# Loading a weight matrix by three transfers over 128 partitions instead of four over 32

## The chip, the cores and the metric

The kernel runs on one core of a Trainium2 chip. A core has five engines that run side by side: TensorE (PE) multiplies matrices, VectorE (DVE), ScalarE (ACT) and GpSimd (POOL) work on elements, and SyncE (SP) issues transfers. Each has its own list of instructions, worked off in order; semaphores hold one until another's result is there. Data lie in a memory of 128 partitions (SBUF). Transfers between it and the main memory (DRAM) are carried out by 16 DMA engines, which all issuing engines share. The metric is the device time of one execution in microseconds (us).

## What is computed

A gated linear attention runs over 4 x 8 sequences of 768 steps with heads of 48; its output, as 3072 tokens of 384, goes through a feed-forward block with two weights, 384 x 2048 and 2048 x 384:

```python
for t in range(S):
    state = alpha[:, :, t, :, None] * state + np.einsum('bhd,bhe->bhde', k[:, :, t], v[:, :, t])
    y[:, :, t] = np.einsum('bhd,bhde->bhe', q[:, :, t], state)
x = y.transpose(0, 2, 1, 3).reshape(B * S, H * D)
h = x @ w_in
g = h * np.clip(h + 3.0, 0.0, 6.0) / 6.0
out = g @ w_out
```

q, k, v and alpha are float32. Both weights are float64, so each of their numbers is moved as two 32-bit words, and the kernel makes float32 of them on the chip.

## The kernel before

The 3072 tokens are 24 chunks of 128 (six per batch), and two chunks are a group. For a chunk the kernel loads alpha, k, q and v (lines 263 to 297), makes running products of alpha (lines 335 and 346), scores, the part within the chunk and the part from the state (lines 395 to 544), and puts the result, transposed, into xT (line 546). For a group the feed-forward block follows: from group 2 on by the products of a fast matrix scheme (line 685 for the first weight, line 785 for the second), in the first two groups in the plain way, because the weights are still coming in: ff1 (line 559, matmuls in line 564) and ff1_half (line 568, line 575) for the first weight, ff2 (line 597, line 602) for the second.

The order of all steps is written out by hand as one long string of words (from line 831 on); a word is a step's short name with its arguments, and each engine gets its instructions in that order. `w.i` is load_weight(i), `d1.i`, `d2.i`, `dx.i`, `d3.i` and `d4.i` decode a slice (round_low on ACT, line 207; magnitude on ACT, line 217; sign on ACT, line 212; high_bits on DVE, lines 224 to 231; add_low on POOL, line 238), `f.g.i.m` is ff1 of group g on the first weight's slice i, and `fa`, `fb` are its two halves. `la`, `lk`, `lq` and `lv` load alpha, k, q and v of a chunk.

Each weight comes in eight slices (NSL = 768 numbers for each of 128 partitions). Slices 0 to 7 are the first weight: slice i is its columns 256 i to 256 i + 255, all 384 rows. The row 96 p + 32 t + r (p under 4, t under 3, r under 32) belongs in partition 32 p + r, place t; a piece of a row is 256 numbers of 8 bytes, 2 KB in one run. A slice lands in a raw buffer (five for these slices, used in turn, HOMES in line 162), is decoded into w1, and the buffer is loaded again. Slices 8 to 15 are the second weight, with 128 partitions in one transfer of 3 KB runs (line 187).

All these loads are issued by SP, in the written order. From the first slice to the last of the first weight it is: w.1, the loads lq.2, lk.2 and lk.3, w.0, lq.3 and lv.2 (two transfers), w.3, w.4, w.5, w.2, la.5, lq.5, la.4 and lv.4 (two transfers), w.6, w.7; then lq.4 and the second weight from w.8 on. Some wait: w.5 until POOL has used the buffer of slice 0, w.7 until it has used that of slice 2, lk.3, lv.2, lq.5 and lv.4 until PE is done with the old contents. Each transfer also counts on one of eight semaphores in turn, and waits for the transfer eight before it, which used the same one. On PE the first uses of the slices come in the order 1, 0, 3, 4, 2, 5, 6, 7; after `f.1.5.0` and a transpose the order is

```
f.1.0.3 f.1.6.2 f.1.7.0 f.0.7.3 f.0.6.2
```

and after these the second weight is used, from `b.1.0` on.

Of the kernel before, what the change touches and what calls it, by code (L numbers as in the profile page):

```python
# [17 lines left out]
def kernel(  # L18
# [32 lines left out]
    nc = tc.nc  # L51
# [5 lines left out]
    NP = H // 2  # L57
    DF = moe_w_out.shape[0]
    KT = DM // C
# [38 lines left out]
    for r in range(max(NR, NV)):  # L98
        for name, pad, n in (("a", 1.0, NR), ("k", 0.0, NR), ("q", 0.0, NR), ("v", 0.0, NV)):
            if r >= n:  # L100
                continue
            if name == "v":
                t = consts.tile([C, H, 64], FP, tag=f"v{r}")
            else:
                t = rings[:, 3 * r + "akq".index(name)]
# [12 lines left out]
    for r in range(2):  # L118
        t = consts.tile([C, NP * W + 1], FP, tag=f"ax{r}")
        nc.vector.memset(t, 0.0)  # L120
        aX.append(t)
        t = consts.tile([C, NP * W], FP, tag=f"ini{r}")
# [8 lines left out]
    for r in range(2):  # L131
        t = consts.tile([C, NP, 2 * D], FP, tag=f"st{r}")
        nc.gpsimd.memset(t, 0.0)
        st.append(t)
    for r in range(2):
        t = consts.tile([C, NP, 2 * D], FP, tag=f"sm{r}")
# [27 lines left out]
    def raw_of(i):  # L164
        return raws[HOMES[i]]

    def weight_dst(i):
        if i < NW1:
            n = NSL // KT
            return w1[:, :, i * n : (i + 1) * n]  # L170
        m = NSL // DM
        return w2[:, (i - NW1) * m : (i - NW1 + 1) * m, :]

    def load_weight(i):
        u = 2 if wide else 1
        dst = weight_dst(i)
        m = dst.shape[1]
        to = raw_of(i).rearrange("p (m n) w -> p m (n w)", m=m) if wide else dst
        if i < NW1:
            n = NSL // KT  # L180
            src = moe_w_in[:, u * i * n : u * (i + 1) * n].rearrange(
                "(p t r) f -> p r t f", p=NP, t=KT)
            for p in range(NP):
                nc.sync.dma_start(out=to[32 * p : 32 * p + 32], in_=src[p])
        else:
            o = (i - NW1) * m * C
            nc.sync.dma_start(
                out=to, in_=moe_w_out[o : o + m * C, :].rearrange("(f p) n -> p f n", p=C))
# [468 lines left out]
    for i in range(8):  # L657
        r, o = divmod(i, 3)
# [70 lines left out]
    t = {1: b[0, 1], 2: spare[:, 0], 3: spare[:, 1], 4: spare[:, 2]}  # L729
# [73 lines left out]
    def store2(g, i):  # L803
# [6 lines left out]
    steps = {  # L810
        "la": lambda j: load_akq("a", j), "lk": lambda j: load_akq("k", j),
        "lq": lambda j: load_akq("q", j), "lv": load_v, "w": load_weight,
        "d1": round_low, "d2": magnitude, "dx": sign, "d3": high_bits, "d4": add_low,
        "ta": lambda j: transposed("a", j), "tk": lambda j: transposed("k", j),
# [182 lines left out]
```

## Time and profile before

| | |
|---|---|
| median of 3 runs | 563.11 us (562.15 to 563.6) |
| the profiled execution, its own time | 562.15 us |
| its span, first to last instruction | 560.4 us |
| PE busy in 0 to 10, 10 to 20, 20 to 30 us | 8.54, 9.36, 9.20 us |
| PE busy in each 10 us from 30 to 110 us | 10.00 us |
| first weight: transfers in the trace | 24 to raw buffers, 8 to a buffer that lies in g_sb, 192 KB each |
| one issue of them on SP, median | 428 ns (311 to 1811) |
| from issue to landing, median | 4.6 us (3.3 to 6.5) |
| all transfers from 10 to 56 us | 9.11 MB, 198 GB/s, 92% of 16 engines |

The page gives each engine's busy time, then the span in 40 slices of 14 us, in which a digit is the busy share in tenths. A row of a timeline is start, duration, engine, line and operation, and in brackets how long the engine stood before it and what ended that. A row of windows is a stretch, its length, the busy time (and count) of PE, of PE's weight loads, DVE, ACT and POOL, then the granted clock of TensorE (1.00 is full), the mean busy share of the DMA engines and GB/s. A row of DMA packets is their count and bytes; behind the queue's name stand packets, MB and the time that the packets took as a share of 16 engines over the stretch. Packets of one engine can overlap, so that share can pass 100%. "SPq" is SP's queue of transfers.

### The profile page before, as it was taken

To read this page: it belongs to the slowest core of one execution; us is meant where nothing else is said; L and a number is where in the kernel's file an instruction comes from. 1 tells how busy PE (TensorE), PEld (TensorE's weight loads), DVE (VectorE), ACT (ScalarE), POOL (GpSimd) and SP (SyncE) were. 2 spreads that over 40 slices of the span, in tenths; PEclk is the share of its full clock that TensorE was granted. 3 is DMA by queue.
4 is the path that set the end of the run, shared out by engine and by line. 5 is a ranking of instruction groups with operands and counts; after the bars stand their busy time and mean duration, and the time that the engine had idled before them with its cause. 6 is when DMAs were issued, how large, how long until landed. Compare 5 with 4: busy or idle time off the path is not lost.

```text
span 560.4 us, 14913 instructions
## 1 busy us (share of the span) xinstructions
PE 548.9 (98%) x6222; PEld 511.3 (91%) x6222; DVE 470.3 (84%) x822; ACT 210.3 (38%) x382; POOL 55.1 (10%) x76
## 2 busy tenths in 40 slices
PE   8999999999999999999999899999999999999997
PEld 8789876799899899999999799999999999999997
DVE  6979897999999899999998589999789777484570
ACT  2676671104523424322333242442333422542420
POOL 3343346000000000000000000000100100000000
PEclk9999999999999999999999999999999999999999
DMA  8997679311305344445424544253125040000000
GB/s 175 211 205 177 187 225 209 87 36 30 90 8 138 89 96 96 111 117 113 133 59 107 122 109 103 70 137 80 48 65 114 4 126 1 9 15 15 9 15 29
DMA packets 98516, 52.83 MB, mean 94 GB/s; under 512 B 51472, under 2 KB 91664, under 8 KB 98448
## 3 DMA queue, kind: packets, MB, share of 16 engines
q1 hardware_dynamic: 91824, 47.15, 35.9%
q10 hardware_dynamic: 6624, 4.72, 2.6%
q8 instruction: 49, 0.80, 0.6%
q14 instruction: 19, 0.16, 0.1%
HBM read 43.71 MB, written 8.13 MB: 93 GB/s over the span
## 4 chain that ended last, share of the span: by engine, by line
PE 80%; DVE 8%; SPq 5%; DMA 4%; issue 2%; ACT 0%; POOL 0%; DVEq 0%; ACTq 0%; POOLq 0%
PE m_ps L785 30%; PE m_ps L685 26%; PE m_ps L564 6%; PE m_ps L602 4%; SPq L292 2%; PE m_ps L575 2%; PE y_ps L543 2%; SPq L277 2%; PE sc_ps L377 1%; DMA kq<-in_k_dram 1%; PE y_ps L523 1%; PE sc_ps L402 1%; PE m_ps L617 1%; SPq L460 1%; PE y_ps L527 1%
## 5 line engine op out<-in xcount | busy, mean ns | idle before, releaser
L785 PE MATMUL m_ps<-w,g_sb 128*128 128x192 f32 x704 | 121.8, 327 | 1.2 <-DVE g_sb L626 0.8
L785 PEld LDWEIGHTS m_ps<-w,g_sb 128*128 128x128 f32 x704 | 113.8, 190 | 2.7 <-DVE g_sb L626 1.0
L691 ACT COPY g_sb<-m_ps 128x512 f32<-128x512 f32 x110 | 64.2, 584 | 127.7 <-PE m_ps L685 121.3
L785 PE MATMUL m_ps<-rings,g_sb 128*128 128x192 f32 x528 | 92.6, 329 | 0.0
L685 PE MATMUL m_ps<-xc,w 128*128 128x128 f32 x640 | 84.2, 279 | 2.9 <-DVE oh L801 2.5
L785 PEld LDWEIGHTS m_ps<-rings,g_sb 128*128 128x128 f32 x528 | 86.6, 193 | 0.2 <-DVE g_sb L626 0.2
L580 ACT ACTIVATE r<-g_sb,half 128x512 f32<-128x512 f32 x80 | 57.2, 722 | 69.0 <-DVE g_sb L626 29.1
L685 PEld LDWEIGHTS m_ps<-xc,w 128*128 128x128 f32 x640 | 78.1, 192 | 5.3 <-DVE oh L801 2.7
L584 DVE SCALAR_TENSOR_TENSOR g_sb<-r,g_sb 128x512 f32<-128x512 f32 x80 | 55.4, 697 | 12.1 <-ACT r L580 8.4
L465 POOL TENSOR_TENSOR t<-t,R 128x384 f32<-128x384 f32 x20 | 19.9, 994 | 368.9 <-DVE t L503 137.5
L685 PE MATMUL m_ps<-xT,raw 128*128 128x128 f32 x400 | 52.9, 277 | 0.0
L685 PEld LDWEIGHTS m_ps<-xT,raw 128*128 128x128 f32 x400 | 49.2, 192 | 0.5
L685 PE MATMUL m_ps<-xT,w 128*128 128x128 f32 x320 | 43.5, 281 | 0.0
L732 DVE TENSOR_TENSOR g_sb<-g_sb 128x512 f32<-128x512 f32 (+1 forms) x55 | 41.7, 789 | 0.2
L685 PEld LDWEIGHTS m_ps<-xT,w 128*128 128x128 f32 x320 | 38.9, 191 | 1.8 <-ACT g_sb L691 0.2
L622 DVE TENSOR_TENSOR g_sb<-g_sb 128x512 f32<-128x512 f32 x40 | 26.9, 680 | 12.3 <-ACT g_sb L691 12.1
L564 PE MATMUL m_ps<-xT,w 128*128 128x256 f32 x144 | 32.3, 381 | 0.0
L685 PE MATMUL m_ps<-xc,raw 128*128 128x128 f32 x240 | 32.1, 278 | 0.0
L335 DVE TENSOR_TENSOR_SCAN R<-t,ones 128x516 f32<-128x516 f32 x24 | 29.7, 1238 | 2.4 <-ACT t L326 2.0
L564 PEld LDWEIGHTS m_ps<-xT,w 128*128 128x128 f32 x144 | 26.9, 190 | 3.7 <-issue 0.2
L685 PEld LDWEIGHTS m_ps<-xc,raw 128*128 128x128 f32 x240 | 29.6, 191 | 0.6
L346 DVE TENSOR_TENSOR_SCAN P<-t 128x516 f32<-128x516 f32 x24 | 29.7, 1238 | 0.2
(126 smaller groups left out, 734.5 us busy)
## 6 DMA issues: line engine op xcount, KB each, us to landing
raw<-in_moe_w_out_dram SPq DMA_DIRECT2D x8, 768.0 KB, 4.5
raw<-in_moe_w_in_dram SPq DMA_DIRECT2D x24, 192.0 KB, 4.4
out_dram<-oh ACTq DMA_DIRECT2D x44, 96.0 KB, 1.8
qq<-in_q_dram SPq DMA_DIRECT2D x36, 96.0 KB, 2.6
aq<-in_alpha_dram SPq DMA_DIRECT2D x36, 96.0 KB, 2.5
kq<-in_k_dram SPq DMA_DIRECT2D x36, 96.0 KB, 2.6
far<-kq SPq DMA_DIRECT2D x13, 256.0 KB, 2.2
kb<-far SPq DMA_DIRECT2D x52, 64.0 KB, 2.3
```

Source lines behind the costliest of these rows:

```text
L335: nc.vector.tensor_tensor_scan(out=reverse(R, n - 1, n), data0=reverse(ax, n, n), data1=reverse(ones, n, n), initial=0.0, op0=ALU.mult, op ...
L346: nc.vector.tensor_tensor_scan(out=P_t[j], data0=aX[j % 2][:, 0:n], data1=ini[j % 2], initial=0.0, op0=ALU.mult, op1=ALU.add)
L465: nc.gpsimd.tensor_tensor(out=st[j % 2], in0=sm[j % 2], in1=R_t[j][:, :, 0:1].to_broadcast([C, NP, 2 * D]), op=ALU.mult)
L564: nc.tensor.matmul(h[:, f], w1[:, kk, o : o + C], xT_t[g][:, kk], start=(kk == 0), stop=(kk == KT - 1))
L580: nc.scalar.activation(out=to, in_=h, func=AF.Relu, bias=half, scale=1.0 / 6.0)
L584: nc.vector.scalar_tensor_tensor(out=to, in0=r, scalar=1.0, in1=h, op0=ALU.min, op1=ALU.mult)
L602: nc.tensor.matmul(o_t[c], gs[0][:, f, c * C : (c + 1) * C], w2[:, f], start=(f == 0), stop=(f == NF - 1))
L622: eng.tensor_tensor(out=out, in0=in0, in1=in1, op=ALU.add if s1 > 0 else ALU.subtract)
L685: nc.tensor.matmul(acc[g][i][:, f * C : (f + 1) * C], spots[w][:, f * C : (f + 1) * C], x_of(g, x), start=(first and f == 0), stop=last, s ...
L691: nc.scalar.copy(out=slots[z], in_=acc[g][i])
L732: nc.vector.tensor_tensor(out=out, in0=in0, in1=in1, op=ALU.subtract)
L785: nc.tensor.matmul(to[g], a, rhs[:, f], start=(first and f == 0), stop=(last and f == HF - 1), skip_group_check=True)
```

## The change

A slice of the first weight is cut in another way. Before, there is one transfer for each p: 32 partitions, and in each of them three runs of 2 KB. After, there is one for each t: 128 partitions, one run of 2 KB in each. The same bytes go to the same places; a slice takes three transfers of 256 KB instead of four of 192 KB. The order of the steps, the buffers and the decoding stay.

```diff
         if i < NW1:
             n = NSL // KT
             src = moe_w_in[:, u * i * n : u * (i + 1) * n].rearrange(
-                "(p t r) f -> p r t f", p=NP, t=KT)
-            for p in range(NP):
-                nc.sync.dma_start(out=to[32 * p : 32 * p + 32], in_=src[p])
+                "(p t r) f -> t p r f", p=NP, t=KT)
+            for t in range(KT):
+                nc.sync.dma_start(out=to[:, t], in_=src[t])
```

In the built program an old transfer reads a pattern of 32 x 3 x 512 words of 4 bytes and writes one of 32 x 3 x 512; a new one reads 4 x 32 x 512 (blocks of 32 rows that lie 96 rows apart) and writes 128 x 1 x 512. The other loads read and write patterns of equal counts, with 32, 64 or 128 in front.

## The prediction

> **What bounds the kernel now.** I read the busy shares first, then the chain of waits, then the slices in time, and then the one stage that the diff touches, the first 60 us.
>
> ```profile
> PE 548.9 (98%) x6222; PEld 511.3 (91%) x6222; DVE 470.3 (84%) x822; ACT 210.3 (38%) x382; POOL 55.1 (10%) x76
> ...
> DMA  8997679311305344445424544253125040000000
> GB/s 175 211 205 177 187 225 209 87 36 30 90 8 138 89 96 96 111 117 113 133 59 107 122 109 103 70 137 80 48 65 114 4 126 1 9 15 15 9 15 29
> ...
> PE 80%; DVE 8%; SPq 5%; DMA 4%; issue 2%; ACT 0%; POOL 0%; DVEq 0%; ACTq 0%; POOLq 0%
> ```
>
> PE is never idle for long, and the chain that ends last runs through it for 80%. A loss on PE in the first 60 us is therefore not recovered later: everything behind it is shifted. The transfers are dense in just the seven slices (of 14 us) in which the weights come in, and this is where the change acts. Next, who feeds whom there (timelines of SP's queue, ACT, POOL and PE, and the source view of line 184):
>
> ```profile
> 10.90 2.12 SPq L184 DMA_DIRECT2D raw<-in_moe_w_in_dram  x4
> 43.47 8.31 SPq L184 DMA_DIRECT2D raw<-in_moe_w_in_dram  x8
> DMA to landing us min/median/max: 3.3/4.6/6.5
> 56.89 0.94 ACT L207 ACTIVATE raw<-raw 128x768 int32<-128x768 uint32 x1 [0.91 <-DMA raw<-in_moe_w_in_dram]
> 61.21 1.47 POOL L238 TENSOR_TENSOR w<-raw 128x768 int32<-128x768 int32 x1 [3.66 <-DVE raw L231]
> 58.12 13.12 PE L564 MATMUL m_ps<-xT,w 128*128 128x256 f32 x60
> ```
>
> The first slice is issued at 10.90. The last one issued (slice 7) has landed by 56.89, when ACT, which had waited 0.91 us for it, starts to decode it. POOL finishes that slice at 61.21 + 1.47 = 62.68. The 60 matmuls of PE are five calls of 2.6 us, in the written order f.1.0, f.1.6, f.1.7, f.0.7, f.0.6 (the chain of waits starts them at 58.29): the first use of slice 7 is at 58.29 + 2 x 2.59 = 63.47. So between landing and use lie 5.8 us of decoding and 0.8 us of slack. A delay of that landing passes on to PE but for 0.8 us.
>
> Last, what a transfer costs on the 16 DMA engines (packets of three stretches):
>
> ```profile
> DMA packets 8616, 1.62 MB, mean 162 GB/s; under 512 B 8616, under 2 KB 8616, under 8 KB 8616
> q1 hardware_dynamic: 8616, 1.62, 84.1%
> ...
> DMA packets 420, 0.69 MB, mean 229 GB/s; under 512 B 87, under 2 KB 87, under 8 KB 420
> q1 hardware_dynamic: 420, 0.69, 105.0%
> ...
> DMA packets 190, 0.58 MB, mean 389 GB/s; under 512 B 0, under 2 KB 0, under 8 KB 190
> q1 hardware_dynamic: 190, 0.58, 96.7%
> ```
>
> From 0 to 10 us only q, k, v and alpha move, in 192-byte packets: 0.841 x 16 x 10 us / 8616 = 15.6 ns each. From 26 to 29 us it is nearly all the first weight, in 2 KB packets: 1.05 x 16 x 3 us = 50.4 us, less 87 x 15.6 ns, over 333 packets = 147 ns each. From 69.5 to 71 us it is the second weight, in 3 KB packets over all 128 partitions: 0.967 x 16 x 1.5 us / 190 = 122 ns, which is 25 GB/s for one engine, or 81 ns for 2 KB.
>
> **The change, part by part.** Everything outside line 184 stays in its order; PE's instruction list is the same one. Eight slices, four transfers each, become eight slices of three: 32 issues become 24. The 3072 packets of 2 KB (384 rows x 8 slices) stay.
>
> *Issue.* An issue of line 184 takes 428 ns now. In the new form the two sides of a transfer no longer have the same counts: the source is 4 blocks of 32 rows, the destination 128 partitions in one step. No transfer of before is like that. The nearest rows are the 0.43 us of the matching patterns and the 0.60 us of the slowest steady form (line 292). I take 0.60: 24 x 0.60 - 32 x 0.43 = +0.6 us over 40 us of SP's queue. It lies beside the moving of the data, which takes far longer; without that cover it would be 0.6 us. SP issues in order, and by the program each transfer waits for the one eight before it. What stands behind line 184 on SP are the next q, k, alpha and v loads and then the second weight. 24 and 32 are both multiples of eight, so later transfers keep their partners.
>
> *Spread.* This decides. In every transfer of before, source and destination have the same leading count, 32, 64 or 128, which 16 engines divide evenly. In the new one the leading counts are 4 and 128. The only cut that both sides share at their outer step is into 4 blocks of 32 partitions. So I expect four engines to carry each slice, and always the same four, because nothing in the pattern distinguishes one transfer from the next. The trace cannot show it; the other bound is that all 16 work (the second rival). Four engines then move 3072 / 4 = 768 packets each, where 16 moved 192.
>
> [...]
>
> *Time of a packet.* Four engines pull at most a quarter of what 16 do, and write over all partitions, so the second weight's 81 ns is the nearest row; the far end is the 147 ns of the 32-partition form, if the four get in each other's way as the 16 do today. I take 100 ns, a little under a third of the way, since the four walk through their 32 partitions at the same pace and will meet at times.
>
> [...]
>
> *Sum.* The queue of the busiest engine, from the first new transfer: 2.4 us between issue and landing that is not packets (the 3.3 us of the shortest, less its 6 packets of 147 ns), eight slices of 96 packets, and between them seven loads of q, k or alpha (64 packets of 15.6 ns on an engine, 1.0 us each) and four of v (0.5 us): 9.0 us. Slice 7 lands at 10.9 + 2.4 + 9.0 + 768 x 0.100 = 99.1 instead of 56.9: +42.2. For 81 ns it is +27.6, for 147 ns +78.3. The engines don't run dry in between: slice 5 waits until slice 0 is decoded and slice 7 until slice 2 is. Two slices (over 15 us), and four loads with a slice (over 11 us), stand in the queue meanwhile, against some 6 us of decoding and 2.4 us of latency.
>
> PE takes the delay over less its 0.8 us of slack: +41.4. Then there is a start after standing still. At 317 us PE stood for 2.5 us, and after it the granted clock fell:
>
> ```profile
> 320.00:324.00 4.00, 3.07 (x14) 3.08 (x15) 3.93 (x7) 1.03 (x3) 0.00 (x0) 0.68 0.45 112
> 324.00:328.00 4.00, 4.00 (x29) 4.00 (x28) 2.17 (x5) 0.90 (x2) 0.00 (x0) 0.89 0.31 56
> ```
>
> That is (0.32 + 0.11) x 4 = 1.7 us of clock lost once, after the last stall; earlier ones cost nothing, as PE waits there anyhow. Behind slice 7 the decoding of the second weight follows at its old pace (POOL's additions come each 3.7 us), so nothing comes back: +43.1 us. The profiled execution took 562.15 with a span of 560.4, and is the fastest of three whose median is 563.11. 562.15 + 43.1 = 605.3, about 606 as a median. By 81 ns it is 591, by 147 ns 641.
>
> **The rivals.** *Four engines in step*: they meet at every packet, each takes 147 ns, and the time is 641. For it: equal queues started together; the 147 ns row shows that engines can hold each other up by two thirds. Against it: any one delay of a few hundred ns takes them apart.
>
> *All 16 engines work* (the other side: not slower): the pattern is dealt by rows after all, and a packet takes 81 instead of 147 ns, 192 x 66 ns = 12.7 us less on each engine. It decides if the dealing goes by the destination's 128 alone. Little of it reaches the end, because PE is full once the weights flow:
>
> ```profile
> 20.00:30.00 10.00, 9.20 (x135) 7.57 (x134) 9.85 (x16) 8.01 (x10) 4.85 (x4) 1.00 1.09 229
> 30.00:40.00 10.00, 10.00 (x197) 8.48 (x196) 8.40 (x15) 7.22 (x11) 4.25 (x4) 1.00 0.86 198
> 40.00:50.00 10.00, 10.00 (x60) 9.07 (x60) 7.59 (x9) 8.73 (x14) 5.05 (x3) 1.00 0.81 167
> ```
>
> Before 30 us PE idles 0.8 us in this stretch and 0.64 in the one before: at most 1.4 us to win, less up to 0.6 us of issue. Time 562 to 563.
>
> *Four engines, but hidden*: the loads land late and something absorbs it. ACT's wait of 0.91 us and the 0.8 us of slack leave room for 2 us at most; only another order of the loads gives more, which the diff doesn't make. At half the forecast's loss, 563.1 + 21 = 584.
>
> **How the numbers follow.** Forecast (four engines, 81 to about 120 ns) 0.62, in step 0.23, all 16 engines 0.10, hidden 0.05. The range 588 to 642 goes from just under 81 ns to 147 ns; outside it are the 16 engines (0.10), the hidden case (0.05) and what is above 642 (0.05). A difference under 0.3% (1.7 us) can't be told from none, as the three runs spread by 1.45 us. Faster 0.04 and same 0.06 share the 16-engine case, 562 to 563; slower 0.90 is the rest.
>
> **What will show it.** While the first weight loads, the mean DMA share falls from 0.9 or more to about a quarter, and the rate from 200 GB/s to 60 to 110; the median landing of line 184 grows from 4.6 us to some 20 (eight transfers in flight, each 32 packets of 100 ns per engine). ACT's first instruction on slice 7 moves from 56.9 to about 99, PE shows gaps between the calls of line 564 and a lower clock behind them, and from f.1.7 on everything is shifted by one amount. The prediction is wrong if the DMA share stays at 0.9 with landings of 3 to 4 us (16 engines), if the share is a quarter but PE moves less than 20 us, or if packets take over 150 ns.

## The result and the profile after

| | before | after |
|---|---|---|
| median (four runs each, on the same chip) | 562.63 us (562.11 to 563.6) | 594.73 us (593.68 to 596.69) |
| ratio | | 1.0572, 95% interval 1.0538 to 1.0607 |
| span of the profiled execution | 560.4 us | 594.9 us |

The change makes the kernel 5.7% slower, about 32 us. The profiled execution after is the slowest of its four (596.69), so its span shows 34.5 us. First the page of the changed kernel: busy shares, slices, chain of waits.

```profile
PE 558.3 (94%) x6222; PEld 518.4 (87%) x6222; DVE 470.1 (79%) x822; ACT 209.1 (35%) x382; POOL 54.3 (9%) x76
...
PEclk9879798999999999999999998999999999999999
DMA  7422445793122143434452354425213222000000
...
PE 71%; DMA 10%; SPq 7%; DVE 7%; ACT 2%; issue 1%; POOL 0%; DVEq 0%; ACTq 0%; POOLq 0%
```

PE's share falls from 98% to 94% and the chain now runs for 10% through transfers instead of 4%. The loss arises at the start: the DMA digits there, 8 9 9 7 6 7 9 before, are 7 4 2 2 4 4 5 now, and the clock row is no longer all nines. The lines that answer to those shown before, from the source view of line 184, the timelines of ACT, POOL and PE, the waits of PE in the first stretch, and one piece of the chain of waits:

```profile
L184 SPq DMA_DIRECT2D raw<-in_moe_w_in_dram x18: 531/566/5448, 10.8 to 75.8; - x18
91.06 0.91 ACT L207 ACTIVATE raw<-raw 128x768 int32<-128x768 uint32 x1 [6.84 <-DMA raw<-in_moe_w_in_dram]
95.32 1.47 POOL L238 TENSOR_TENSOR w<-raw 128x768 int32<-128x768 int32 x1 [9.02 <-DVE raw L231]
91.34 1.11 PE L308 MATMUL tq_ps<-ident,rings 128*128 128x128 f32 x4 [8.20 <-DMA rings<-in_q_dram]
92.24 14.42 PE L564 MATMUL m_ps<-xT,w 128*128 128x256 f32 x60
PE tq_ps L308 <- DMA rings<-in_q_dram: 18.8, 4, 8.2
76.42 14.88 DMA rings<-in_q_dram
```

The four transposes of line 308, before the change:

```profile
57.69 0.60 PE L308 MATMUL tq_ps<-ident,rings 128*128 128x128 f32 x4
```

Slice 7 reaches ACT at 91.06 instead of 56.89, 34.2 us later. POOL ends it at 96.79 instead of 62.68, 34.1 later. The block of 60 matmuls starts 34.1 us later (92.24 instead of 58.12) and lasts 14.42 instead of 13.12 us. What PE waited for, however, is not the decoding of slice 7, but the load of q for chunk 4, which stands behind slice 7 in SP's queue (8.20 us, and 18.8 us over four such loads). It lands 14.9 us after the start of its issue, where no load of line 266 took more than 6.6 us before, and the transposes that need it start at 91.34 instead of 57.69.

What the DMA engines did from 36 to 46 us, while nearly nothing but the first weight moved:

```profile
DMA  3222222222222232522222222222232222222222
...
DMA packets 488, 0.99 MB, mean 99 GB/s; under 512 B 14, under 2 KB 14, under 8 KB 486
q1 hardware_dynamic: 486, 0.97, 25.9%
```

The share of 16 engines is 25.9%, which is four engines at work all the time. The others were not idle for want of issues: from 32.0 to 68.9 us SP goes from one issue to the next, and single issues of line 184 last up to 5.4 us there. When that longest one began, at 41.7 us, the transfer eight before it (v, line 297) had made its last mark on their semaphore at 35.3; what holds an issue no view shows. 0.259 x 16 x 10 us, less 14 x 15.6 ns, over 472 packets is 87 ns for 2 KB. The trace also holds each packet by itself. Of the time in which 2 KB packets of the first weight were under way, exactly four were so for 71%, and five, as packets of one engine can overlap, for 14%; the median of the 3072 packets is 84 ns, the mean 91. Before the change it was most often 16 at once (20% of the time, and 17 for 16%), and median and mean were 140 ns.

### The profile page after: what moved, and what is told of

The parts are those of the page before. It is cut to its first block, busy times and chain, and to the rows that moved or that the text cites. A ratio compares the mean times of both kernels' runs of the same rounds, so it can differ in the third digit from the quotient of the medians.

```text
span 594.9 us, 14887 instructions
## 1 busy us (share of the span) xinstructions
PE 558.3 (94%) x6222; PEld 518.4 (87%) x6222; DVE 470.1 (79%) x822; ACT 209.1 (35%) x382; POOL 54.3 (9%) x76
## 4 chain that ended last, share of the span: by engine, by line
PE 71%; DMA 10%; SPq 7%; DVE 7%; ACT 2%; issue 1%; POOL 0%; DVEq 0%; ACTq 0%; POOLq 0%
PE m_ps L785 29%; PE m_ps L685 26%; DMA raw<-in_moe_w_in_dram 4%; PE m_ps L602 4%; PE m_ps L564 3%; DMA rings<-in_q_dram 3%; SPq L184 3%; SPq L277 2%; PE y_ps L543 2%; DMA kq<-in_k_dram 2%; PE sc_ps L377 1%; PE y_ps L523 1%; DVE g_sb L584 1%; PE y_ps L527 1%; SPq L292 1%
## 5 line engine op out<-in xcount | busy, mean ns | idle before, releaser
L580 ACT ACTIVATE r<-g_sb,half 128x512 f32<-128x512 f32 x80 | 57.2, 722 | 67.5 <-DVE g_sb L626 28.0
L732 DVE TENSOR_TENSOR g_sb<-g_sb 128x512 f32<-128x512 f32 (+1 forms) x55 | 41.7, 789 | 0.2
L685 PEld LDWEIGHTS m_ps<-xT,w 128*128 128x128 f32 x320 | 38.9, 191 | 1.6 <-issue 0.2
L564 PE MATMUL m_ps<-xT,w 128*128 128x256 f32 x144 | 35.5, 406 | 3.2 <-ACT xT L551 3.2
L564 PEld LDWEIGHTS m_ps<-xT,w 128*128 128x128 f32 x144 | 29.1, 206 | 8.1 <-ACT xT L551 3.6
```

What stands on the lines that cost most here:

```text
L564: nc.tensor.matmul(h[:, f], w1[:, kk, o : o + C], xT_t[g][:, kk], start=(kk == 0), stop=(kk == KT - 1))
L580: nc.scalar.activation(out=to, in_=h, func=AF.Relu, bias=half, scale=1.0 / 6.0)
L685: nc.tensor.matmul(acc[g][i][:, f * C : (f + 1) * C], spots[w][:, f * C : (f + 1) * C], x_of(g, x), start=(first and f == 0), stop=last, s ...
L732: nc.vector.tensor_tensor(out=out, in0=in0, in1=in1, op=ALU.subtract)
```

## The experiments

**How many engines, and by what.** The theory: the number of engines is set by the count in front of the source's pattern, 4 in the changed kernel. The rival: the new form as such is slow, by unequal counts on its two sides or by its size. Four kernels keep three transfers of 256 KB over 128 partitions and change that count; all other instructions stay. The rows of the first weight so come to other partitions, and these four compute another output by the same work.

```diff
-                "(p t r) f -> t p r f", p=NP, t=KT)
+                "(p t r) f -> t p r f", p=2, t=KT)
```

(8 and 16 in the second and third; in the fourth `"(t r) f -> t r f", t=KT`.)

> The changed kernel's three transfers per slice over 128 partitions, but the source is 2 blocks of 64 rows (row 192 b + 64 t + r) instead of 4 blocks of 32; the rows of the first weight so come to other partitions, and the result is another one. Theory (the leading count of the source, the smaller of the two, is the number of engines that work): 1536 packets of 91 ns on each of two engines, last slice of the first weight on ACT at 10.9 + 2.4 + 9.0 + 139.8 = 162, about 105 us later than before; DMA share near 2/16 while it loads; time 660 to 675 us. Rival (the new form itself is slow, by its unequal counts or its size, whatever the count in front): the same as the changed kernel, 590 to 600 us.

> As the run with 2 blocks, but 8 blocks of 16 rows (row 48 b + 16 t + r); rows of the first weight at other partitions, so another result. Theory: 384 packets on each of eight engines, 34.9 us at 91 ns, last slice on ACT at 57.2, where it was 56.9 before the change; DMA share near one half; time 562 to 567 us. Rival (the form itself): 590 to 600 us.

> As the run with 2 blocks, but 16 blocks of 8 rows (row 24 b + 8 t + r); rows of the first weight at other partitions, so another result. The counts of the two sides are still unequal (16 and 128). Theory: all 16 engines, 192 packets each, DMA share as before the change, time 560 to 564 us, and no more than 1.4 us under the kernel before, since PE is full from 30 us on. Rival (unequal counts are slow): 590 to 600 us.

> Three transfers per slice over 128 partitions with 128 rows in one block (row 128 t + r), so equal counts on both sides; rows of the first weight at other partitions, so another result. Theory: all 16 engines, packets of about 85 ns instead of 147, so that the first weight loads at well over 230 GB/s, yet the time stays at 560 to 564 us, as the loads are no longer what PE waits for. Rival (a better spread over the partitions is worth its 12.7 us of engine time): 548 to 556 us. Rival (three transfers of 256 KB are slower than four of 192 KB for their size): 590 to 600 us.

| count in front | time, us | ratio to before (561.98), 95% interval | DMA share of a stretch with little else |
|---|---|---|---|
| 2 | 656.0 | 1.1665 (1.1611 to 1.172) | 13.1% |
| 4 (the change) | 594.73 | 1.0572 (1.0538 to 1.0607), against 562.63 | 25.9% |
| 8 | 563.24 | 1.0013 (0.9987 to 1.0038) | 56.2% |
| 16 | 561.4 | 0.9993 (0.9968 to 1.0017) | 80.6% (24 to 27 us) |
| 128 | 559.76 | 0.9974 (0.9948 to 1.0) | 87.1% (24 to 27 us) |

With 2 blocks, the packets from 52 to 62 us and ACT's first instruction on slice 7:

```profile
DMA packets 251, 0.53 MB, mean 53 GB/s; under 512 B 4, under 2 KB 4, under 8 KB 249
q1 hardware_dynamic: 249, 0.50, 13.1%
149.93 0.90 ACT L207 ACTIVATE raw<-raw 128x768 int32<-128x768 uint32 x1 [14.00 <-DMA raw<-in_moe_w_in_dram]
```

13.1% is 2.1 engines of 16, and 0.131 x 160 us / 249 is 84 ns a packet. With that in the prediction's sum: 22.3 + 1536 x 0.084 = 151.3; measured 149.93. My expectation used 91 ns and came out at 162, and 660 us at the least instead of 656, a miss by the size of the packet. With 8 blocks, the packets from 30 to 40 us and slice 7 again:

```profile
DMA packets 1407, 1.99 MB, mean 199 GB/s; under 512 B 493, under 2 KB 493, under 8 KB 1404
q1 hardware_dynamic: 1404, 1.95, 56.2%
59.62 0.91 ACT L207 ACTIVATE raw<-raw 128x768 int32<-128x768 uint32 x1 [1.43 <-DMA raw<-in_moe_w_in_dram]
```

Eight engines would be 50%; the 493 small packets of other loads, at 15.6 ns each, are 4.8%. Slice 7 comes 2.7 us later than before the change (57.2 expected), and the time can't be told from the time before. With 16 blocks the counts are still unequal, the issue costs 0.60 us as in the run with 8, and nothing is lost:

```profile
L184 SPq DMA_DIRECT2D raw<-in_moe_w_in_dram x18: 536/597/1381, 10.2 to 51.0; - x18
```

Packet by packet it is the same: with 2 blocks two packets of the first weight are under way at once for 88% of the time, with 8 blocks seven to nine for 81%, with 16 blocks 13 to 17 for 57%. So the rival falls: neither unequal counts nor 256 KB nor the dearer issue cost anything that can be told here; the count in front does. The trace doesn't name the engines, so which four work was not seen, only how many.

The run with 128 rows in one block also tells what the spread over all partitions is worth with all engines at work. From 36 to 46 us:

```profile
DMA packets 5017, 2.32 MB, mean 232 GB/s; under 512 B 4275, under 2 KB 4275, under 8 KB 5016
q1 hardware_dynamic: 5016, 2.30, 87.9%
```

0.879 x 160 us, less 4275 x 15.6 ns, over 742 packets: 100 ns for 2 KB, where the old form took 147. I had expected 85; packet by packet, the median is 84 ns and the mean 103. The median falls by 2.2 us, with an interval that just reaches no change. Part of that is the mix of runs: between runs of the same mean granted clock (1.00, or 0.997) it is about 1 us (means of 559.2 against 560.3, and of 561.5 against 562.6). The rival of 548 to 556 us falls.

**How much of the delay reaches the end.** The new form for one slice, the other seven as before:

```diff
-        if i < NW1:
+        if i == 1:
+            n = NSL // KT
+            src = moe_w_in[:, u * i * n : u * (i + 1) * n].rearrange(
+                "(p t r) f -> t p r f", p=NP, t=KT)
+            for t in range(KT):
+                nc.sync.dma_start(out=to[:, t], in_=src[t])
+        elif i < NW1:
```

> The new form for the first loaded slice (slice 1) alone, the seven others as before. Theory: four engines take 96 x 91 ns = 8.7 us for it where 16 took 24 x 147 ns = 3.5; the q and k loads behind it in the queue come 5.2 us later and PE waits for them by about 3 us; some of that is absorbed where the engines run dry later, so the time is 563 to 566 us. Rival (only the total of the eight slices counts, each an eighth): +4.0 us, 566 to 568.

> The new form for the last loaded slice (slice 7) alone, the seven others as before. Theory: 5.2 us later on ACT, less 0.8 us of slack, plus up to 1.7 us of lower clock after the stall: time 566 to 570 us, and more than with the first slice alone. Rival (the loads run ahead of PE and one slice is hidden): 562 to 564 us.

The first loaded slice alone: 564.98 us, ratio 1.006 (1.0031 to 1.0089), +2.6 us. The last alone: 568.43 us, ratio 1.0112 (1.0074 to 1.015), +6.0 us. Both lie in the expected ranges. With the first alone, ACT starts on its slice 3.3 us later (22.31 instead of 18.97), PE stands 3.6 us for a load of q behind it, and the block of 60 matmuls starts 3.6 us later (61.67 instead of 58.12). With the last alone, from the timelines of ACT and PE (line numbers are six higher here):

```profile
62.05 0.90 ACT L213 ACTIVATE raw<-raw 128x768 int32<-128x768 uint32 x1 [6.36 <-DMA raw<-in_moe_w_in_dram]
62.31 1.11 PE L314 MATMUL tq_ps<-ident,rings 128*128 128x128 f32 x4 [4.76 <-DMA rings<-in_q_dram]
```

Slice 7 comes 62.05 - 56.89 = 5.2 us later, the amount expected for 96 packets on four engines in place of 24 on each of 16. PE stands 4.8 us, and for the q load behind the slice. The delay of the first slice costs half of the 5.2 us by which its transfers were reckoned longer; of the last one's nothing is absorbed.

**Whether PE waits for that q load or for the slice.**

```diff
-  ... st.4 lq.4 fb.2 ...
+  ... st.4 fb.2 ...
-  ... d2.2 dx.2 w.6 d3.2
+  ... d2.2 dx.2 lq.4 w.6 d3.2
```

> The changed kernel with one word moved: the load of q of chunk 4 stands ahead of slice 6 in the queue instead of behind slice 7. In the changed kernel's trace PE stood 8.2 us for that load before the calls of slice 0, 6 and 7. Theory (the load only lands with slice 7, and PE would wait for slice 7 next): PE starts slices 0 and 6 earlier, and slice 7 is used at about 97 us instead of 98; gain 0 to 2 us, time 592 to 595. Rival (that load is what costs): 8 us less, 585 to 588.

596.48 us, ratio 1.061 (1.058 to 1.0641), which overlaps the change's own interval: nothing gained, and the expected 592 to 595 us missed. PE's waits up to 165 us and its timeline:

```profile
PE tq_ps L308 <- DMA rings<-in_q_dram: 9.4, 3, 5.3
PE m_ps L564 <- POOL w L238: 6.3, 1, 6.3
...
97.28 10.75 PE L564 MATMUL m_ps<-xT,w 128*128 128x256 f32 x36 [6.30 <-POOL w L238]
```

The 8.2 us before chunk 4's transposes are gone, and PE stands 6.3 us for POOL's end of slice 7 instead. Between the load of q and the first use of slice 7 stand two calls on PE, 5.2 us at full clock, and decoding the slice takes about as long (from 91.51 on ACT to 97.22 here); so with the wait for q gone, the slice holds PE. PE then reaches slice 7 somewhat earlier, at 97.28, but the three calls from there on take 10.75 us where three of 2.59 us are 7.8 (the granted clock is 0.50 from 96 to 102 us), and they end at 108.03 instead of 106.66. That clock is what my expectation left out. The rival, 8 us less, falls.

**The old transfers in another order.**

```diff
-            for p in range(NP):
+            for p in (0, 2, 1, 3):
```

> The kernel before with the four transfers of a slice in the order 0, 2, 1, 3 of their partition blocks, so that transfers that follow each other lie in different halves of the 128 partitions. All 16 engines work in either order. Theory (the engines go through a transfer in step, and PE is full once the weights flow): no change, 561 to 564 us. Rival (transfers in two halves overlap, and packets become shorter): packets under 120 ns, and up to 1.4 us less.

562.39 us, ratio 0.9998 (0.9975 to 1.0021): no change, as expected. The mean packet of the first weight takes 131 ns instead of 140, not the rival's less than 120.

**The same output with 128 rows in one block.** Here x is laid out so that a transfer may take 128 rows in one run of partitions, with the loads of the run with 128 rows. One state product (pair 0, last block) takes all 128 rows instead of 64, and the product of 64 rows that it ran beside is left alone. Before, these products overlap: 24 matmuls of 0.27 to 0.30 us each (line 543) take 0.81 us together. The diff gives the main lines.

```diff
-        return ps_t["y%d" % (kk // 2), j][32 * p : 32 * p + 32, kk % 2]
+        i = 3 * p + kk
+        return ps_t["y%d" % (i // 8), j][32 * (i % 4) : 32 * (i % 4) + 32, i // 4 % 2]
...
-        for p, kk, r in parts + [(p, 1, slice(0, C)) for p in range(NP)]:
+        parts.pop(1)
+        whole = [(p, 1, slice(0, C)) for p in range(NP)] + [(0, 2, slice(0, C))]
+        for p, kk, r in parts + whole:
```

> A version that computes the same output with 128 rows in one block: block i = 3 p + kk of 32 features goes to partitions 32 (i mod 4), place i div 4 of x, so that row 128 t + r of the first weight belongs in partition r, place t. Three transfers per slice over 128 partitions with equal counts. [...] Theory: all 16 engines; the loads give what the run with 128 rows gave, about 2 us, and the one product that no longer runs beside its partner costs 0.05 to 0.15 us in each of 20 chunks, 1 to 3 us: 559 to 565 us, no clear change. Rival (the spread over partitions was worth it): 556 us or less.

> As the run with three transfers and 128 rows in one block, with one transfer of 768 KB per slice instead of three. Theory: 8 issues instead of 24 save some 7 us of SP's queue, which nothing waits for; the same time as with three, within 2 us. Rival (issues matter): 3 us or more below it.

563.13 us, ratio 1.0041 (1.0022 to 1.006), against 561.15 for the kernel before; with one transfer per slice 565.11 us, 1.0067 (1.0044 to 1.0091). The state products of one chunk, before and in the run with three transfers (chain of waits):

```profile
353.98 0.73 PE y_ps L543 x24
```

```profile
353.99 0.95 PE y_ps L554 x24
```

The product that has lost its partner costs 0.22 us (I had said up to 0.15), in 20 chunks 4.4 us. The loss of some 2 us would so be 4.4 less what the loads gain, the 1 to 2 us seen with 128 rows above; the two parts were not measured apart, and the sum is met only roughly. Neither version beats the kernel before. The two with one and three transfers have overlapping intervals; what one large transfer costs was not followed further.

## Why the prediction was right

*What bounds the kernel.* Right: a delay in the first 60 us is not recovered. The first products of line 785, in the chain of waits before and after:

```profile
107.02 15.60 PE m_ps L785 x96
```

```profile
142.45 15.60 PE m_ps L785 x96
```

They start 35.4 us later, and the span ends 34.5 later. The 0.9 us between them came back and were not traced; the prediction had nothing coming back.

*Issue.* Taken as 0.60 us and hidden; the runs with 8 and 16 blocks show 0.60 us, and lose nothing by it.

*Spread.* Right, and this was the step that decided: 25.9% of 16 engines. That there would be four was the author's estimate from the pattern alone, as no transfer before the change had unequal counts. The runs with 2, 8 and 16 blocks show that the count in front sets it here: 13.1%, 25.9% and 56.2%, the last less 4.8% of small packets, are 2.1, 4.1 and 8.2 engines of 16. The rival with all 16 engines falls.

*Time of a packet.* The term that was mis-sized: 100 ns taken, 87 measured. The nearest row (81) was the better one; the third of the way towards 147 was too much, and the case of engines in step, 641 us, did not occur. The forecast of 606 us was so 11 us too high, and the time came nearer to the 591 of that row; the wide range held both. That engines hold each other up when they meet was the author's reading of 147 ns against 81 (81% more, not two thirds), two rows that differ in run length and in the number of partitions; no run shows that cause. At 87 ns, with a median of 84, no such loss is seen among the four. Whether they were out of step, or met without a loss, no run tells.

*Sum.* 22.3 + 768 x 0.087 = 89.1 against 91.06 on ACT (with the mean of 91 ns it is 92.2), so the rest of the sum was right to 2 us. With 100 ns it said 99.1, and 42.2 us of delay instead of 34.2. This one term makes up most of the difference between 606 and 595. The landing of some 20 us can't be checked by a median, as the trace gives none; the longest pieces of loads in the chain of waits are 10.8, 14.2 and 14.9 us.

*How it reaches PE.* Half right. I let PE wait for slice 7 alone, and passed over the q load that follows it in the same queue, though I had listed the loads that stand behind line 184. PE waited for that load. The amount came out nearly the same, since the load lands with the slice, and with the load moved away PE waits for the slice; that the omission cost the forecast nothing is luck. The transposes start 33.7 us later, where the forecast by the slice's measured delay, 34.2 less 0.8 of slack, is 33.4.

*Clock.* 1.7 us named; 1.3 seen in the block behind the last stall (14.42 against 13.12), and 0.5 in the transposes ahead of it (1.11 against 0.60).

*The rivals.* Hidden loads: two slices of eight, taken alone, cost 2.6 and 6.0 us, so they are not hidden; even the first loses half of its 5.2. All 16 engines: what it would have given is seen in the run with 128 rows, 2.2 us between medians and about 1 us at the same clock, where I had said 1.4 at most.

## What to carry to other kernels

Before reshaping a transfer, write down the pattern of both its sides as the instruction carries it, and look at the count in front: here a DRAM pattern that begins with 4 blocks kept the transfer on 4 of 16 engines, though the other side has 128 partitions. The loads that stood behind the delayed ones in SP's queue came late with them; ask of each of them who waits, not only of the one that was changed. And a faster load is worth only what its reader waits for: here a third off the packet time gave 1 to 2 us of 562.

## What was not expected of the hardware

With two or four engines at work a packet of 2 KB takes 84 to 87 ns, nearly the same as the 81 ns worked out from the second weight: no loss of one engine by another is seen. Over 128 partitions the median packet takes 84 ns with 2, 4, 8, 16 and 128 in front alike; in the old form over 32 partitions it takes 140 ns. And the lower clock comes back with one stall after the other: from 20 to 100 us the granted clock of PE lies below full in each stretch of 10 us, for instance

```profile
70.00:80.00 10.00, 9.39 (x57) 9.11 (x58) 6.87 (x9) 4.66 (x7) 3.64 (x2) 0.78 0.40 110
```

(0.78 here, 0.76 to 0.90 in the others), but only what follows the last stall lies on the path: after the earlier ones PE soon waits again, and the chain of waits runs through the loads.
